# A two-dimensional FFT and a SwiGLU block on one core: buffers drawn by the build-time scheduler, its ScalarE lengths and its priorities set anew

## The chip, the cores and the metric

The kernel runs on one core of a Trainium2 chip. Its time is the device time in microseconds; three runs took 612.49, 616.39 and 612.35 us, with a median of 612.49 us. The engines are TensorE (PE, with its weight loads as PEld), VectorE (DVE), ScalarE (ACT), GpSimd (POOL) and SyncE (SP), which issues the DMAs.

## The reference

```python
def _attn_ref(x):                      # x: (8, 3008, 256) float32
    X = np.fft.fft(x, axis=1)
    X = np.fft.fft(X, axis=2)
    return X.real.astype(np.float32)

def _moe_ref(x, w_gate, w_val, w_out): # x: (24064, 256), w_gate, w_val: (256, 1536), w_out: (1536, 256)
    g = x @ w_gate
    silu = g * (1.0 / (1.0 + np.exp(-g)))
    val = x @ w_val
    return (silu * val @ w_out).astype(np.float32)
```

The real part of a two-dimensional transform of each of the eight batches, reshaped to 24064 rows, goes through a gated feed-forward block.

## The kernel before

**The mathematics in use.** The real part of the transform of a real input has a mirror symmetry. The kernel therefore computes 12032 columns (half the rows of the result) as two parts, `Pt` (even) and `Qt` (odd); row k of the result comes from P + Q and the mirrored row from P - Q. The hidden axis of 256 is folded into the weights once: `Wp` and `Wq` are the gate and value weights times cosine and sine tables, and `Wm` is a multiple of `Wq` for the mirrored rows.

**Tiles and units.** The columns are cut into 24 tiles of 512 (the first of 480, the fourth too, the last of 320 with 8 extra). Each tile has 12 units (t, f), one per 128 of the 1536 hidden values, so there are 288 units. In every unit TensorE makes a gate tile `g` and a value tile `v` in PSUM (512 columns of fp32, one bank each), ScalarE applies Silu, and products `hp` (row) and `hm` (mirrored row) are written as bf16 for the second product with `Wo`. A unit comes in several forms:

- whole (`whole_a`, `whole_b`): six matmuls; ScalarE makes Silu of g twice, VectorE multiplies into hp and hm.
- split (`part_a`, `part_b`): five matmuls. An even value `es` is put aside (by VectorE at L1068 with the broadcast row `bc`, or, in a seeded unit, by a ScalarE copy at L1066 after ScalarE has written the first row into v at L1017). The mirrored value goes by VectorE (L1129) and the mirrored Silu by ScalarE (L1115) into an `sv` tile that serves two units; GpSimd multiplies the pair into hm (L1136). VectorE multiplies hp (L1139), or, in units named by `POOL` and `POOL_END`, ScalarE copies the value (L1145) and GpSimd multiplies (L1148).
- with the gate split too (`GATE...`): one matmul less; VectorE makes an even gate (L1047) and a mirror gate (L1107).

`SPLIT_EARLY`, `GATE_EARLY` (tiles 1 and 2), `SEED`, `POOL`, `GATE` (tiles 3 to 20, in turns of two) and the `..._END` lists (tiles 21 to 23) say which unit has which form.

**The products with Wo.** `OWork` runs the product of the tile before (L1185: eight blocks of 12 matmuls of 256 columns, eight matmuls per unit), ScalarE evicts a pair of blocks from `o` to `ev` (L1191, L1194), and SP stores it (L1197).

**The transform.** For batch b, GpSimd folds the input `XA`, `XC` in twelve steps each (`fold_step`, L162 to L186: SDf, EOf, Af, then CEa/BBa for A or Fc for C). SP loads the input and spreads Fc to `St`. Then `transform_op` multiplies with the tables into an `o` and a `g` tile (L1341), ScalarE copies o to `od` (L1348), and VectorE adds and subtracts into pieces of Pt and Qt (the puts, L1358 and L1364). The first batch, the tables and the weights are made in a prologue of some 22 us.

**Who orders the work.** Every step is an `Op` in a build-time scheduler, `Sched`: an engine, a duration (`act_us`, `dve_us`, `pool_us`, `pe_us` with additions), a lag to other engines (`LAG`), a due time `at` (TensorE's clock at that point plus a shift such as `SH_OD`), and the tiles it opens (`new`). `run` picks for each engine, within a window of due times (`WINDOW`), the step that can start first, and reckons that a tile takes the earliest buffer to come free (`free`). It then calls the steps in that order, and each engine executes its own in order. Pools: three buffers each for g, v, sp, sg and ev, two each for o, sv and es. What buffer a tile gets is left to the pool of that name, which holds all its buffers.

`spread(("C", 1), 6, 6, 12)` and its like (L1230) place the folds by unit; L1526 puts the loads of A1 at unit 8; `ROW_PE` names the units at which TensorE makes the broadcast row of tiles 1 to 3.

Of the kernel before, what the change touches and what calls it, by code (L numbers as in the profile page):

```python
# [31 lines left out]
def kernel(  # L32
# [45 lines left out]
    stp = ctx.enter_context(tc.tile_pool(name="st", bufs=3))  # L78
    pqp = ctx.enter_context(tc.tile_pool(name="pq", bufs=5))
    odp = ctx.enter_context(tc.tile_pool(name="od", bufs=2))  # L80
    psG = ctx.enter_context(tc.tile_pool(name="psG", bufs=3, space=bass.MemoryType.PSUM))
    psV = ctx.enter_context(tc.tile_pool(name="psV", bufs=3, space=bass.MemoryType.PSUM))
    psO = ctx.enter_context(tc.tile_pool(name="psO", bufs=2, space=bass.MemoryType.PSUM))
    ctx.enter_context(tc.manual_schedule())

    Wp = const.tile([P, 2, Dff], BF16, name="Wp")
# [233 lines left out]
    shift = tp.tile([P, 3], F32, name="shift")  # L320
# [355 lines left out]
    for q in range(2):  # L676
        S, Dd = SC[:, 0, :, q, :], SC[:, 1, :, q, :]
# [14 lines left out]
    sgp = ctx.enter_context(tc.tile_pool(name="sg", bufs=3))
    spp = ctx.enter_context(tc.tile_pool(name="sp", bufs=3))
    svp = ctx.enter_context(tc.tile_pool(name="sv", bufs=2))
    esp = ctx.enter_context(tc.tile_pool(name="es", bufs=2))
    brp = ctx.enter_context(tc.tile_pool(name="br", bufs=1))
    bcp = ctx.enter_context(tc.tile_pool(name="bc", bufs=2))
    evp = ctx.enter_context(tc.tile_pool(name="evO", bufs=3))

    def row_pieces(c0, n, minus):  # L700

# [22 lines left out]
        return out[r0:r0 + step * (n - 1) + 1:step, :]  # L724

    ROW_GAP = 1
    LOAD_AT = 2
    LOADS, LOADS_LATER = 4, 3
    SH_ROW = -4
    ES_BUFS = 2  # L730
    SP_BUFS = 3
    SG_BUFS = 3
    EV_BUFS = 3
    W_PE = 9
    W_ACT = 6.25
    W_DVE = 7.25
    W_POOL = 9
    SH_SEED = 4
    SH_EG = 1.45
    SH_SP = 2.85  # L740
    SH_ES = 3.05
    SH_GM = 0.7
    SH_SM = 3.9
    SH_VM = 2.85
    SH_VAL = 0.85
    SH_HP = 3.15
    SH_HM = 3.75
    SH_EV = 4
    SH_FOLD = 3.15
    SH_OD = -2.3  # L750
    SH_PUT = -1.75
    GRP = 4
    WM_ACT = ((1, 0), (1, 1))
    class Op:
        __slots__ = ("eng", "dur", "lat", "fn", "at", "n", "deps", "owners", "new", "ring", "start", "end", "users")

    LAG = {"DMA": 0.0, "PE": 0.20, "ACT": 0.17, "DVE": 0.15, "POOL": 0.12, "SP": 0.0}
    BUFS = {"g": 3, "v": 3, "o": 2, "sp": SP_BUFS, "sv": 2, "es": ES_BUFS, "sg": SG_BUFS, "ev": EV_BUFS, "od": 2, "h": 2, "bc": 2, "br": 1, "pq": 5, "cp": 2,
            "fc": 1, "st": 3}
    WINDOW = {"PE": W_PE, "ACT": W_ACT, "DVE": W_DVE, "POOL": W_POOL, "SP": 6.0, "DMA": 1e9}  # L760
    PSUM = ("g", "v", "o")

    class Sched:

        def __init__(self):
            self.ops = []
            self.wr, self.rd = {}, {}
            self.live = {p: [] for p in BUFS}
            self.clock = 0.0
# [4 lines left out]
        def add(self, eng, dur, fn, r=(), w=(), new=(), after=(), lat=None, shift=0.0, ring=0.35):  # L774
            o = Op()
            o.eng, o.dur, o.fn, o.n = eng, dur, fn, len(self.ops)
            o.lat = LAG[eng] if lat is None else lat
            o.ring = ring
            o.at = self.clock + shift
            if eng == "PE":  # L780
                self.clock += dur
            o.new, o.deps, o.owners = list(new), set(), set()
            for k in r:
                o.owners.add(k[0])
                if k in self.wr:
                    o.deps.add(self.wr[k])
                same = self.rd.setdefault(k, [])
                if k[0][0] in PSUM:
                    o.deps.update(x for x in same if self.ops[x].eng != eng)
                same.append(o.n)  # L790
            for k in after:
                o.deps.update(self.rd.get(k, ()))
            for k in w:
                o.owners.add(k[0])
                if k in self.wr:
                    o.deps.add(self.wr[k])
                o.deps.update(self.rd.pop(k, ()))
                self.wr[k] = o.n
            o.deps.discard(o.n)
            o.owners.update(o.new)  # L800
            self.ops.append(o)

        def run(self, begin):
            ops = self.ops
            last, queue = {}, {p: [] for p in BUFS}
            for o in ops:
# [3 lines left out]
                for w_ in o.new:  # L810
                    if w_ not in queue[w_[0]] and w_ not in self.live[w_[0]]:
                        queue[w_[0]].append(w_)
            free = {p: [0.0] * (BUFS[p] - len(self.live[p])) for p in BUFS}
            owned = {w_ for p in BUFS for w_ in self.live[p]}
            todo = {}
            for o in ops:
# [7 lines left out]
            ring = 0.0  # L824
# [3 lines left out]
            def ready(o):  # L828
                at = 0.0
                for d in o.deps:  # L830
                    x = ops[d]
                    if x.end is None:
                        return None
                    at = max(at, x.end + (x.lat if x.eng != o.eng or x.eng == "SP" else 0.0 if x.eng == "PE" else 0.03))
                for w_ in o.new:
                    if w_ in owned:
                        continue
                    p = w_[0]
                    if queue[p][0] != w_ or not free[p]:
                        return None  # L840
                    at = max(at, min(free[p]))
                return at

            while left:
                best = None
                floor = min(l[0].at for l in todo.values() if l)
                for e, l in todo.items():
# [22 lines left out]
                s, o = best  # L870
# [4 lines left out]
                if o.eng == "SP":  # L875
                    ring = max(o.end + o.lat, ring + o.ring)
                    o.lat = ring - o.end
                    lanes = lanes[1:] + [ring]
                order.append(o)
                for w_ in o.new:  # L880
                    if w_ not in owned:
                        owned.add(w_)
                        queue[w_[0]].remove(w_)
                        free[w_[0]].remove(min(free[w_[0]]))
                for w_ in o.owners:
                    if w_ in last:
# [13 lines left out]
    def act_us(n):  # L900
        return n / 1200 + 0.055
# [9 lines left out]
    state = {}  # L911
    t_end = tile_of((B - 1) * H) + 1
    FIRST = 3 * nF
    ROW_PE = {13: 1, 22: 2, 36: 3}
    SPLIT_EARLY = ((1, 2), (1, 3), (1, 4), (1, 5), (1, 8), (1, 9), (1, 10), (1, 11), (2, 0), (2, 1), (2, 4), (2, 5), (2, 6), (2, 7), (2, 8), (2, 9), (2, 10), (2, 11))
    GATE_EARLY = ((2, 1), (2, 4))

    SEED = (1, 2, 3, 4, 5, 6, 8, 11, 13, 14, 15, 16, 17, 21, 23)
    SEED_END = (0, 4, 6, 8, 9)
    POOL = (16,)  # L920
    POOL_END = (0, 1, 6, 9)
    GATE = (0, 2, 3, 4, 7, 14, 15, 16)
# [24 lines left out]
    S = Sched()  # L947
# [62 lines left out]
    def seed_op(u):  # L1010
        t, f = u
        w = width(t) + (B if t == nT - 1 else 0)
        kv = (("v", u), 0)

        def fn():
            T_[kv] = psV.tile([P, T], F32, name="v")
            nc.scalar.activation(T_[kv][:, :w], bc[t][:, :w], AF.Copy, scale=w0[:, 1, f:f + 1])  # L1017

        S.add("ACT", act_us(w) + 0.13, fn, r=[(("bc", t), 0)], w=[kv], new=[("v", u)], shift=SH_SEED)

    def part_a(u):
        if whole(u):
# [54 lines left out]
    def part_b(u):  # L1077
        if whole(u):
            return whole_b(u)
        t, f = u  # L1080
        w = width(t)
        wp = w + (B if t == nT - 1 else 0)
        kg, kv, kP, kQ = unit_keys(u)
        ksp, kes, keg, kgm = (("sp", u), 0), (("es", u), 0), (("sg", ("eg", u)), 0), (("sg", ("gm", u)), 0)
        ksv = ("sv", (t, f // 2))
# [134 lines left out]
    bc = {}  # L1220
# [375 lines left out]
```

## Time and profile before

| what | value |
|---|---|
| median of three runs | 612.49 us |
| the profiled execution | 612.9 us, of which 611.1 us are the span from first to last instruction |
| granted TensorE clock | 1.00 in every 20 us stretch up to 600 us, 0.96 in the last 11 us |
| ScalarE waits for TensorE's g (L1043, L1115) | 6.3 and 3.7 us |
| GpSimd's hm waits for sv by VectorE and by ScalarE | 37.4 and 28.9 us |
| first matmul of tile 1 and of tile 3 | 44.7 and 95.5 us |
| last matmul | 607.4 us |
| DMA moved | 57.9 MB, 95 GB/s on average |

Busy times are shares of the span. A matmul's own duration in the rows (some 0.38 us for 512 columns) is longer than the distance to the next one, since matmuls are pipelined; distances are taken from start to start. Some 50 of 4066 matmuls have no row in the trace; a gap of exactly one matmul's time is such a row and no wait.

### The profile page before, as it was taken

What the parts mean: (1) busy time and instruction counts of PE and PEld (TensorE: products, weight loads), DVE (VectorE), ACT (ScalarE), POOL (GpSimd) and SP (SyncE); (2) the same over time, 40 slices, a digit from 0 to 9 for tenths busy, and PEclk for the clock granted to TensorE, in tenths of its full rate; (3) what the DMA queues carried; (4) which work ended last, traced back from release to release, by engine and by line L of the source; (5) the groups of instructions that cost most, each with busy time, mean ns of one, the idle gap of its engine ahead of it and who ended that gap; (6) DMA issues with size and microseconds to landing.
All of it is one profiled execution on the core that took longest, in us unless ns stands there. A gap on an engine that the chain in (4) does not pass through costs nothing.

```text
span 611.1 us, 12629 instructions
## 1 busy us (share of the span) xinstructions
PE 597.0 (98%) x4016; PEld 394.9 (65%) x4072; DVE 575.8 (94%) x1066; ACT 558.6 (91%) x1072; POOL 482.3 (79%) x447
## 2 busy tenths in 40 slices
PE   8999999999999999999999999999999999999997
PEld 6556666666666666566666666666666666666676
DVE  8998899999999999989999999999999999998982
ACT  7697679899999999899999999999899999999993
POOL 8847988999899899978897797987886544457662
PEclk9999999999999999999999999999999999999999
DMA  9966337445517234363261113135211212111112
GB/s 227 146 114 145 97 111 176 123 121 139 149 39 166 76 89 137 106 130 100 57 170 52 53 49 93 53 98 134 59 52 36 62 46 63 36 53 51 53 53 79
DMA packets 51055, 57.92 MB, mean 95 GB/s; under 512 B 7254, under 2 KB 38170, under 8 KB 50988
## 3 DMA queue, kind: packets, MB, share of 16 engines
q1 hardware_dynamic: 47334, 53.97, 33.2%
q0 software_dynamic: 3216, 2.36, 2.9%
q10 hardware_dynamic: 438, 0.77, 0.5%
q8 instruction: 32, 0.52, 0.4%
q14 instruction: 35, 0.29, 0.2%
HBM read 29.43 MB, written 24.65 MB: 88 GB/s over the span
## 4 chain that ended last, share of the span: by engine, by line
PE 65%; ACT 9%; DVE 9%; POOL 9%; issue 5%; DMA 1%; POOLq 0%; ACTq 0%; DVEq 0%
PE o L1185 27%; PE g L945 18%; PE v L945 15%; POOL hm L1136 3%; ACT sv L1115 3%; DVE hp L1139 2%; DVE sv L1129 2%; DVE sg L1047 2%; ACT v L1017 2%; DVE sg L1107 1%; ACT es L1066 1%; DMA XA<-in_moe_w_gate_dram 1%; PE o L1341 1%; PE g L1341 1%; ACT sp L1043 1%
## 5 line engine op out<-in xcount | busy, mean ns | idle before, releaser
L1136 POOL TENSOR_TENSOR hm<-sv 128x1024 bf16<-128x1024 f32 (+2 forms) x135 | 251.2, 1862 | 89.0 <-DVE sv L1129 37.4
L1129 DVE SCALAR_TENSOR_TENSOR sv<-es,v 128x512 f32<-128x512 f32 (+2 forms) x270 | 181.4, 673 | 11.3 <-PE v L945 10.1
L1139 DVE TENSOR_TENSOR hp<-sp,v 128x512 bf16<-128x512 f32 (+2 forms) x249 | 167.6, 674 | 2.1 <-ACT sp L1112 1.5
L1185 PE MATMUL o<-Wo,hm 128*128 128x256 bf16 (+1 forms) x1128 | 165.0, 272 | 0.5
L1185 PE MATMUL o<-Wo,hp 128*128 128x256 bf16 (+1 forms) x1104 | 160.6, 272 | 0.8
L1185 PEld LDWEIGHTS <-hm 128*128 128x128 bf16 (+2 forms) x1140 | 111.9, 98 | 60.9 <-issue 1.3
L1185 PEld LDWEIGHTS <-hp 128*128 128x128 bf16 (+2 forms) x1140 | 111.9, 98 | 57.6 <-issue 2.0
L1115 ACT ACTIVATE sv<-g 128x512 f32<-128x512 f32 (+2 forms) x187 | 125.1, 680 | 5.1 <-PE g L945 3.7
L1043 ACT ACTIVATE sp<-g 128x512 f32<-128x512 f32 (+2 forms) x187 | 117.6, 629 | 10.4 <-PE g L945 6.3
L1017 ACT ACTIVATE v<-bc,w 128x512 f32<-128x512 bf16 (+2 forms) x150 | 108.5, 723 | 1.6 <-DVE hp L1139 0.9
L945 PE MATMUL v<-Pt,Wp 128*128 128x512 bf16 (+2 forms) x288 | 106.2, 374 | 1.7 <-DVE hp L1139 0.6
L945 PE MATMUL g<-Pt,Wp 128*128 128x512 bf16 (+2 forms) x277 | 103.4, 374 | 3.2 <-DVE Qt L1358 2.4
L1066 ACT COPY es<-v 128x512 f32<-128x512 f32 (+2 forms) x150 | 91.9, 613 | 1.6 <-PE v L945 0.5
L945 PE MATMUL g<-Qt,Wq 128*128 128x512 bf16 (+2 forms) x247 | 91.5, 374 | 0.4
L1068 DVE SCALAR_TENSOR_TENSOR es<-bc,w,v 128x512 f32<-128x512 bf16 (+2 forms) x120 | 87.6, 731 | 3.4 <-PE v L945 1.8
L945 PE MATMUL g<-Qt,Wm 128*128 128x512 bf16 (+2 forms) x205 | 76.7, 374 | 0.7 <-ACT sp L1043 0.4
L945 PEld LDWEIGHTS <-Wp 128*128 128x128 bf16 x576 | 56.3, 98 | 30.2 <-DVE Qt L1358 2.2
L945 PE MATMUL v<-Qt,Wm 128*128 128x512 bf16 (+2 forms) x165 | 61.9, 375 | 0.4
L1047 DVE SCALAR_TENSOR_TENSOR sg<-bc,w,g 128x512 f32<-128x512 bf16 (+2 forms) x83 | 61.0, 735 | 1.0 <-PE g L945 0.9
L1191 ACT COPY ev<-o 128x512 f32<-128x512 f32 x89 | 55.3, 621 | 6.4 <-PE o L1185 6.0
L945 PEld LDWEIGHTS <-Wq 128*128 128x128 bf16 x426 | 41.6, 98 | 27.1 <-issue 5.4
L1115 ACT ACTIVATE sv<-sg 128x512 f32<-128x512 f32 (+2 forms) x83 | 58.0, 699 | 0.3 <-POOL hm L1136 0.3
(198 smaller groups left out, 743.6 us busy)
## 6 DMA issues: line engine op xcount, KB each, us to landing
out_dram<-ev SPq DMA_DIRECT2D x96, 128.0 KB
XA<-in_x_dram SPq DMA_DIRECT2D x30, 256.0 KB
XA<-in_x_dram SPq DMA_DIRECT2D x112, 64.0 KB
XC<-in_x_dram SPq DMA_DIRECT2D x30, 120.0 KB
XC<-in_x_dram SPq DMA_DIRECT2D x105, 32.0 KB
bc<-br SPq DMA_DIRECT2D x19, 128.0 KB
St<-Fc SPq DMA_DIRECT2D x12, 128.5 KB
out_dram<-ev SPq DMA_DIRECT2D x12, 120.0 KB
```

The source lines that it names most:

```text
L945: nc.tensor.matmul(ps[:, :n], Wt[:, gv, fs], src[:, :n], start=start, stop=stop, skip_group_check=True)
L1017: nc.scalar.activation(T_[kv][:, :w], bc[t][:, :w], AF.Copy, scale=w0[:, 1, f:f + 1])
L1043: nc.scalar.activation(T_[ksp][:, :w], T_[kg][:, :w], AF.Silu)
L1047: nc.vector.scalar_tensor_tensor(T_[keg][:, :w], bc[t][:, :w], w0[:, 0, f:f + 1], T_[kg][:, :w], op0=Alu.mult, op1=Alu.add)
L1066: nc.scalar.copy(T_[kes][:, :w], T_[kv][:, :w])
L1068: nc.vector.scalar_tensor_tensor(T_[kes][:, :w], bc[t][:, :w], w0[:, 1, f:f + 1], T_[kv][:, :w], op0=Alu.mult, op1=Alu.add)
L1115: nc.scalar.activation(sv()[:, f % 2, w - 1::-1, 1], T_[kgm if by_dve else kg][:, :w], AF.Silu)
L1129: nc.vector.scalar_tensor_tensor(sv()[:, f % 2, w - 1::-1, 0], T_[kes][:, :w], 2.0, T_[kv][:, :w], op0=Alu.mult, op1=Alu.subtract)
L1136: nc.gpsimd.tensor_tensor(hts_(t)[1][:, f - 1:f + 1, :w], sv()[:, :, :w, 1], sv()[:, :, :w, 0], op=Alu.mult)
L1139: nc.vector.tensor_tensor(hts_(t)[0][:, f, :wp], T_[ksp][:, :wp], T_[kv][:, :wp], op=Alu.mult)
L1185: nc.tensor.matmul(st["ps"][:n, j, :], hts[t][minus][:, f, c:c + n], Wo[:, f, :], start=(f == 0), stop=(f == nF - 1))
L1191: nc.scalar.copy(ev[:, 0:len(pair), :], st["ps"][:, 0:len(pair), :])
```

## The change

Five things are edited together. (1) Eight pools are replaced by sets of pools with one buffer each (`Slots`), and `run` keeps the number of the buffer that it reckons with, and sets it before the step is called. (2) Three durations and two lags of the planner: seed 0.13 to 0.134, mirrored Silu 0.035 to 0.069 (split gate) and 0.032, ACT's lag 0.17 to 0.18, DVE's 0.15 to 0.145. (3) All shifts and three windows. (4) Which units are split, seeded, on GpSimd or split in the gate, in tiles 1 and 2 and in the last three. (5) The places of the first folds, of A1's loads and of the row of tile 1. Two assertions are added to the planner.

```diff
-    psG = ctx.enter_context(tc.tile_pool(name="psG", bufs=3, space=bass.MemoryType.PSUM))
...
+    class Slots:
+        def __init__(self, name, n, **where):
+            self.pools = [ctx.enter_context(tc.tile_pool(name=f"{name}{i}", bufs=1, **where)) for i in range(n)]
+            self.at = 0
+        def tile(self, *what, **named):
+            t = self.pools[self.at].tile(*what, **named)
+            self.at = (self.at + 1) % len(self.pools)
+            return t
+    psG = Slots("psG", 3, space=bass.MemoryType.PSUM)
...
+    C1_AT = 7
+    A1_AT = 17
+    C2_AT = 34
+    A1_LOAD = 9
+    ROW_1 = 11
...
-    W_PE = 9
-    W_ACT = 6.25
-    W_DVE = 7.25
+    W_PE = 8.5
+    W_ACT = 6.0
+    W_DVE = 8.5
...
-    SH_SEED = 4
-    SH_EG = 1.45
-    SH_SP = 2.85
-    SH_ES = 3.05
-    SH_GM = 0.7
-    SH_SM = 3.9
-    SH_VM = 2.85
-    SH_VAL = 0.85
-    SH_HP = 3.15
-    SH_HM = 3.75
-    SH_EV = 4
-    SH_FOLD = 3.15
-    SH_OD = -2.3
-    SH_PUT = -1.75
+    SH_SEED = 2.75
+    SH_EG = 3.25
+    SH_SP = 1.55
+    SH_ES = 2.85
+    SH_GM = -4
+    SH_SM = 3.25
+    SH_VM = 4
+    SH_VAL = 0.0
+    SH_HP = 4
+    SH_HM = 1.05
+    SH_EV = 2.6
+    SH_FOLD = 1.45
+    SH_OD = -3.75
+    SH_PUT = -4
...
+    SLOTS = {"g": psG, "v": psV, "o": psO, "sp": spp, "sv": svp, "sg": sgp, "es": esp, "ev": evp}
...
-            free = {p: [0.0] * (BUFS[p] - len(self.live[p])) for p in BUFS}
+            free = {p: [(0.0, i) for i in range(len(self.live[p]), BUFS[p])] for p in BUFS}
...
+                        held[w_] = min(free[w_[0]])[1]
                         free[w_[0]].remove(min(free[w_[0]]))
+                        o.slots.append((w_[0], held[w_]))
...
             for o in order:
+                for p, i in o.slots:
+                    if p in SLOTS:
+                        SLOTS[p].at = i
                 o.fn()
...
-    SPLIT_EARLY = ((1, 2), (1, 3), (1, 4), (1, 5), (1, 8), (1, 9), (1, 10), (1, 11), (2, 0), (2, 1), (2, 4), (2, 5), (2, 6), (2, 7), (2, 8), (2, 9), (2, 10), (2, 11))
-    GATE_EARLY = ((2, 1), (2, 4))
+    SPLIT_1 = (0, 1, 2, 3, 4, 5, 6, 7, 8, 9)
+    SPLIT_2 = (0, 1, 2, 3, 4, 5, 8, 9)
+    GATE_2 = (0, 2, 4, 6, 7, 9)
...
-    SEED_END = (0, 4, 6, 8, 9)
+    SEED_END = (4, 5, 7, 10)
...
-    POOL_END = (0, 1, 6, 9)
-    GATE = (0, 2, 3, 4, 7, 14, 15, 16)
-    GATE_END = (0, 3, 6)
+    POOL_END = (0, 6, 7, 9, 10)
+    GATE = (0, 2, 4, 5, 7, 14, 15, 16)
+    GATE_END = (0, 4, 7, 9)
```

A unit of tile 2 has its gate split if it is in both `GATE_2` and `SPLIT_2` (0, 2, 4 and 9). Also changed, though not shown: `SH_ROW` from -4 to 0.15.

More of the change, by code (lines that the diff above doesn't have):

```diff
@@ L80 @@
     odp = ctx.enter_context(tc.tile_pool(name="od", bufs=2))
-    psG = ctx.enter_context(tc.tile_pool(name="psG", bufs=3, space=bass.MemoryType.PSUM))
-    psV = ctx.enter_context(tc.tile_pool(name="psV", bufs=3, space=bass.MemoryType.PSUM))
-    psO = ctx.enter_context(tc.tile_pool(name="psO", bufs=2, space=bass.MemoryType.PSUM))
+    class Slots:
[7 more added lines that the diff above has]
+    psG = Slots("psG", 3, space=bass.MemoryType.PSUM)
+    psV = Slots("psV", 3, space=bass.MemoryType.PSUM)
+    psO = Slots("psO", 2, space=bass.MemoryType.PSUM)
     ctx.enter_context(tc.manual_schedule())
@@ L691 @@
     hp = ctx.enter_context(tc.tile_pool(name="ht", bufs=2))
[L692 to L695, printed above, removed]
+    sgp = Slots("sg", 3)
+    spp = Slots("sp", 3)
+    svp = Slots("sv", 2)
+    esp = Slots("es", 2)
     brp = ctx.enter_context(tc.tile_pool(name="br", bufs=1))
     bcp = ctx.enter_context(tc.tile_pool(name="bc", bufs=2))
-    evp = ctx.enter_context(tc.tile_pool(name="evO", bufs=3))
+    evp = Slots("evO", 3)
     def row_pieces(c0, n, minus):
@@ L726 @@
     ROW_GAP = 1
+    C1_AT = 7
[3 more added lines that the diff above has]
+    ROW_1 = 11
+    ROW_2 = 22
+    ROW_3 = 36
     LOAD_AT = 2
     LOADS, LOADS_LATER = 4, 3
-    SH_ROW = -4
+    SH_ROW = 0.15
     ES_BUFS = 2
@@ L754 @@
     class Op:
-        __slots__ = ("eng", "dur", "lat", "fn", "at", "n", "deps", "owners", "new", "ring", "start", "end", "users")
-    LAG = {"DMA": 0.0, "PE": 0.20, "ACT": 0.17, "DVE": 0.15, "POOL": 0.12, "SP": 0.0}
+        __slots__ = ("eng", "dur", "lat", "fn", "at", "n", "deps", "owners", "new", "ring", "slots", "start", "end", "users")
+    LAG = {"DMA": 0.0, "PE": 0.20, "ACT": 0.18, "DVE": 0.145, "POOL": 0.12, "SP": 0.0}
     BUFS = {"g": 3, "v": 3, "o": 2, "sp": SP_BUFS, "sv": 2, "es": ES_BUFS, "sg": SG_BUFS, "ev": EV_BUFS, "od": 2, "h": 2, "bc": 2, "br": 1, "pq": 5, "cp": 2,
@@ L784, in add @@
                 o.owners.add(k[0])
+                assert k in self.wr or k[0][0] != "bc", k
                 if k in self.wr:
@@ L793, in add @@
             for k in w:
+                assert not (k[0][0] in ("pq", "bc") and self.rd.get(k)), k
                 o.owners.add(k[0])
@@ L812, in run @@
                         queue[w_[0]].append(w_)
-            free = {p: [0.0] * (BUFS[p] - len(self.live[p])) for p in BUFS}
+            free = {p: [(0.0, i) for i in range(len(self.live[p]), BUFS[p])] for p in BUFS}
+            held = {w_: i for p in BUFS for i, w_ in enumerate(self.live[p])}
             owned = {w_ for p in BUFS for w_ in self.live[p]}
@@ L840, in ready @@
                         return None
-                    at = max(at, min(free[p]))
+                    at = max(at, min(free[p])[0])
                 return at
@@ L879, in run @@
                 order.append(o)
+                o.slots = []
                 for w_ in o.new:
@@ L890, in run @@
                             ends = [x.end + x.lat for x in ops if x.end is not None and w_ in x.owners]
-                            free[w_[0]].append(max(ends))
+                            free[w_[0]].append((max(ends), held[w_]))
             for o in order:
+                for p, i in o.slots:
+                    if p in SLOTS:
+                        SLOTS[p].at = i
                 o.fn()
@@ L913 @@
     FIRST = 3 * nF
-    ROW_PE = {13: 1, 22: 2, 36: 3}
-    SPLIT_EARLY = ((1, 2), (1, 3), (1, 4), (1, 5), (1, 8), (1, 9), (1, 10), (1, 11), (2, 0), (2, 1), (2, 4), (2, 5), (2, 6), (2, 7), (2, 8), (2, 9), (2, 10), (2, 11))
-    GATE_EARLY = ((2, 1), (2, 4))
+    ROW_PE = {ROW_1: 1, ROW_2: 2, ROW_3: 3}
+    SPLIT_1 = (0, 1, 2, 3, 4, 5, 6, 7, 8, 9)
+    SPLIT_2 = (0, 1, 2, 3, 4, 5, 8, 9)
+    GATE_2 = (0, 2, 4, 6, 7, 9)
     SEED = (1, 2, 3, 4, 5, 6, 8, 11, 13, 14, 15, 16, 17, 21, 23)
-    SEED_END = (0, 4, 6, 8, 9)
+    SEED_END = (4, 5, 7, 10)
     POOL = (16,)
-    POOL_END = (0, 1, 6, 9)
-    GATE = (0, 2, 3, 4, 7, 14, 15, 16)
-    GATE_END = (0, 3, 6)
+    POOL_END = (0, 6, 7, 9, 10)
+    GATE = (0, 2, 4, 5, 7, 14, 15, 16)
+    GATE_END = (0, 4, 7, 9)
     def whole(u):
-        return u[0] < 3 and u not in SPLIT_EARLY
+        return u[0] < 3 and u[1] not in ((), SPLIT_1, SPLIT_2)[u[0]]
     def seeded(u):
@@ L939, in gate_split @@
         if u[0] < 3:
-            return u in GATE_EARLY
+            return u[0] == 2 and u[1] in GATE_2 and u[1] in SPLIT_2
         return u[0] % 2 * nF + u[1] in GATE if u[0] < t_end else u[1] in GATE_END
@@ L1017, in fn @@
             nc.scalar.activation(T_[kv][:, :w], bc[t][:, :w], AF.Copy, scale=w0[:, 1, f:f + 1])
-        S.add("ACT", act_us(w) + 0.13, fn, r=[(("bc", t), 0)], w=[kv], new=[("v", u)], shift=SH_SEED)
+        S.add("ACT", act_us(w) + 0.134, fn, r=[(("bc", t), 0)], w=[kv], new=[("v", u)], shift=SH_SEED)
     def part_a(u):
@@ L1120, in part_b @@
             S.add("ACT", act_us(wp), silu, r=[kg], w=[ksp], new=[ksp[0]], shift=SH_SP)
-            S.add("ACT", act_us(w) + 0.035, silu_m, r=[kgm], w=[ksm], new=[ksv], shift=SH_SM)
+            S.add("ACT", act_us(w) + 0.069, silu_m, r=[kgm], w=[ksm], new=[ksv], shift=SH_SM)
         else:
-            S.add("ACT", act_us(w) + 0.035, silu_m, r=[kg], w=[ksm], new=[ksv], shift=SH_SM)
+            S.add("ACT", act_us(w) + 0.032, silu_m, r=[kg], w=[ksm], new=[ksv], shift=SH_SM)
         def v2():
@@ L1228, in spread @@
         seq.extend((lo + (i * (hi - lo)) // (n - 1), what, i) for i in range(n))
-    spread(("C", 1), 6, 6, 12)
-    spread(("A", 1), 12, 14, 24)
-    lo = 30
+    spread(("C", 1), 6, C1_AT, C1_AT + 6)
+    spread(("A", 1), 12, A1_AT, A1_AT + 10)
+    lo = C2_AT
     for b in range(2, B, 2):
@@ L1525 @@
             loads.extend((("C", 1), k, fn) for k, fn in enumerate(load_c(1, nc.sync)))
-        if i == 8:
+        if i == A1_LOAD:
             loads[0:0] = ((("A", 1), k, fn) for k, fn in enumerate(load_a(1, nc.sync)))
```

## The prediction

> **What bounds the kernel now.** First the busy times, then the same by 20 us stretches, then the starts of single matmuls where TensorE lags.
>
> ```profile
> PE 597.0 (98%) x4016; PEld 394.9 (65%) x4072; DVE 575.8 (94%) x1066; ACT 558.6 (91%) x1072; POOL 482.3 (79%) x447
> ```
> ```profile
> 160.00:180.00 20.00, 19.89 (x131) 12.83 (x132) 19.92 (x35) 19.44 (x38) 19.55 (x17) 1.00 0.22 64
> ...
> 240.00:260.00 20.00, 18.54 (x119) 11.55 (x119) 19.29 (x34) 18.42 (x37) 19.48 (x18) 1.00 0.45 120
> ...
> 280.00:300.00 20.00, 19.02 (x127) 12.44 (x129) 19.31 (x35) 18.55 (x36) 18.94 (x18) 1.00 0.20 56
> ```
>
> The columns of the stretches are span, busy time of PE, PEld, DVE, ACT, POOL, granted clock, DMA share and GB/s. TensorE bounds: 512 columns start every 0.216 us and 256 every 0.109, without gaps, in nearly every stretch (19.89 of 20 is as full as a row gets). Its idle 14.1 us are 3.1 in the first 40 us, 3.4 behind the last matmul, and a few waits between. VectorE is nearly as full (20.00 of 20 in four stretches).
>
> What the waits between are for is seen at 281.55 us:
>
> ```profile
> 279.57 0.92 DVE L1358 TENSOR_TENSOR Qt<-g,od 128x64 bf16<-128x64 f32 x4
> ...
> 279.75 0.60 ACT L1112 ACTIVATE sp<-g 128x512 f32<-128x512 f32 x1
> ...
> 281.33 0.17 DVE L1358 TENSOR_TENSOR Qt<-g,od 128x12 bf16<-128x12 f32 x1
> ...
> 281.55 0.39 PE L945 MATMUL g<-Pt,Wp 128*128 128x512 bf16 x1 [0.82 <-DVE Qt L1358]
> ```
>
> The new `g` tile takes the PSUM buffer of a transform, whose last read (the 12-column put) ends at 281.50. The buffer that ScalarE had read was free at 280.35. In the built program's addresses the shared pool hands buffers out by another rule than the planner, which reckons with the earliest free one. I went through all g, v and o tiles in this way, with the last read of every buffer from the trace: TensorE stood for a later-freed buffer at 107.1 (0.43 us), 255.7 (0.92), 256.9 (0.71, a `v`), 281.5 (0.93), 355.5 (0.31), 426.9 (0.93), 500.9 (0.32) and twice for 0.07 to 0.08: 4.7 us. At 113.4 ScalarE stood 1.2 us for an `sp` buffer that GpSimd still read while another was free, and TensorE lost 0.60 us behind it at 114.1. Together 5.3 us.
>
> **The change part by part.** *Matmuls.* The new lists of split and gate units take away five: four g<-Qt,Wm of 512 columns and one of 320. 4 x 0.216 + 0.136 = **-1.0 us**, all on TensorE's path.
>
> *Buffers by the planner.* The 5.3 us is the most, zero the least. VectorE limits it: the distance from one instruction's start to the next is at least 0.597 us (L1129, L1139, L1107) and 0.657 (L1068, L1047), and with these its work is 47.2 of the 48.2 us between the tile starts at 266.2 and 314.4, where TensorE waits 0.99. Without that wait both would be full. The stretches 167.8 to 217.1 and 314.4 to 364.0 already hold 49.3 and 49.5 us of VectorE work in 49.2 and 49.6. New waits are also possible. A transform's g tile is held from 1.3 to 3.3 us from its last matmul to its last put; at the old holds, the distances in the new order leave ten of 30 transforms short, by 2.1 us in all (the old order leaves five short, by 3.7). Higher priority of od and puts (SH_OD, SH_PUT) should shorten holds, and the hp that stood between two 7-put groups' puts is gone twice. I take two thirds of 5.3: **-3.5 us**; bounds 0 and -5.3.
>
> *Tile 1.* All units 0 to 9 are now split; before, 0, 1, 6 and 7 were whole. A pair of split units fills one of two `sv` buffers, and a GpSimd product (hm) empties it. GpSimd before:
>
> ```profile
> 49.63 2.35 POOL L162 TENSOR_TENSOR SDf<-XC 128x1020 f32<-128x1020 f32 x1 [12.01 <-DMA XA<-in_x_dram]
> ...
> 54.31 1.10 POOL L172 TENSOR_TENSOR Af<-EOf 128x516 f32<-128x516 f32 x1
> ...
> 58.13 0.73 POOL L1457 MEMSET Tab<- 64x752 bf16 x1
> 58.91 0.73 POOL L1458 MEMSET Tab<- 64x756 bf16 x1
> 59.72 3.75 POOL L1136 TENSOR_TENSOR hm<-sv 128x1024 bf16<-128x1024 f32 x2
> 63.43 2.35 POOL L162 TENSOR_TENSOR SDf<-XA 128x1020 f32<-128x1020 f32 x1
> ```
>
> The fold of C1 starts when its last copy within XC lands. That copy now stands one XA load earlier on SP's queue; issue distances there are 0.4 us, so I leave 49.5. The new order puts hm of units 0 and 1 between EOf and Af: 54.2 to 56.1. The rest of the fold (3.8 us) and the two memsets (1.6) follow, and only then hm of units 2 and 3: 61.5 to 63.4. Units 6 and 7 write the buffer that this hm reads. Their first matmuls end at 58.4 to 58.6 in matmul time counted from tile 1's start (44.7), and an sv write starts some 1.4 us later in the rows of before, so at 59.9; it would now start at 63.4. Both writers stand in ScalarE's and VectorE's queues in the plain order of units, and behind them everything of these engines waits. The g tile of unit 9 takes the buffer that ScalarE's write frees (there are three, all in use): due on TensorE at 61.0, free at 63.4 + 0.65 + 0.2 = 64.2. Cost between 0 and 3.3; nearest to the row sums, **+3.0 us**.
>
> *Moved places.* C1, A1 and C2 folds start one, three and four units later, the row of tile 1 two units earlier. A1's coefficients were written at 80.9 and first used at 88.7. With hm products first and TensorE later too, the sums of GpSimd rows put them near 87 and the use near 91: 0. For batch 2 written 151.6, used 153.0; the same sum comes out level, about 154 both: 0, bounds 0 and +4.5 (rival 3).
>
> *Other engines.* VectorE gains five even gates, five mirror gates and three even values, and loses three products: 6.0 us. Of this 3.5 us lie in the last three tiles, where it idles 5.4 us of 40 (17.95 and 16.66 of 20), and the rest in tiles 1 and 2, where it idles 2.4 of 20 and 0.5 to 1.1 of 20: 0, at most +0.5. ScalarE loses 1.6 us, GpSimd gains 3.4 at the end, where it idles 6 of 20. The last tile's product of unit 10 moves to GpSimd; the closing 36 matmuls from 599.5 reach it 1.1 us in, about when it is written: 0 to +0.6, I take 0.1. The new ScalarE lengths only move the plan. The prologue draws the same buffers in the same turn: 0.
>
> **Sum.** -1.0 - 3.5 + 3.0 + 0.1 = -1.4 us. The profiled execution took 612.9 us (span 611.1), so 611.5 of its like; the median of the runs shown is 0.4 lower: **611.1 us**.
>
> **Rivals.**
> 1. *The wait in tile 1 is not met.* For: VectorE was idle 2.4 us of 20 there, and the copy stands earlier. Against: GpSimd's rows have no gap from 49.6 on. -1.0 - 3.5 = 608.0; with the whole 5.3 us 606.2.
> 2. *The buffers bring nothing*, because VectorE is full or because the plan's ends miss the real ones and a later-freed buffer is still drawn. For: VectorE at 100% in two stretches out of four. Against: VectorE stood idle 0.4 us for TensorE right behind the waits at 281.5 and 426.9. -1.0 + 3.1 = 614.6.
> 3. *Slower: GpSimd's chain to batch 2.* Products are now put ahead of fold steps (SH_HM 1.05 for 3.75), so GpSimd may stand for an sv where it would have folded. A product waited 0.66 us on average (89.0 us over 135). If nine of the products up to 151 us gain such a wait, batch 2's coefficients come 6 us later, and TensorE waits for them at 153; the 1.4 us of slack go first. This decides from 1.4 us of added GpSimd idle time. 611.1 + 4.5 = 615.6. For: GpSimd is busy 19.84 and 19.67 of 20 from 100 to 140. Against: its work up to there hardly changes.
> 4. *The clock.* The wait in tile 1 would be the longest of TensorE; the longest now is 1.4 us at 13.5, and the granted clock is 1.00 in every stretch up to 600 us. The first 52 matmuls of 128 columns took 5.38 us, 103 ns each, nearly what 256 columns take later. Should the array fall back to such a pace for 5 us, half of them is lost: 611.1 + 2.6 = 613.7. [...]
>
> **Chances.** Forecast 0.42, rival 1 0.25, rival 2 0.15, rival 3 0.12, rival 4 0.06. The range runs from rival 1 with most of its buffers, 606.5, to rival 3, 616.0. 1% is 6.1 us, about what a measurement here tells from no change: under 606.4 lies only the end of rival 1 (0.08), over 618.6 the end of rival 3 (0.05), the rest is 0.87.
>
> **What would show it.** Right: no TensorE wait of 0.9 us near 255, 281 and 427, a PE wait of about 3 us at 61 with ScalarE's and VectorE's sv writes waiting for hm, GpSimd's second hm not before 61, VectorE at 99% of the stretches that had 97%. Wrong: no wait at 61, or waits at the old places for a put or an sv write, or a transform's matmul that waits for CEa.

## The result and the profile after

The changed kernel took **605.65 us** (median of four runs, 605.42 to 606.99) beside 612.62 us of the kernel before on the same chip: a ratio of 0.9877, 95% interval 0.9836 to 0.9917. In a later series it took 604.99 us beside 613.02: 0.9862, interval 0.9841 to 0.9883. It is some 7 to 8 us faster, just more than 1%. The prediction was 611.1 us with a range from 606.5 to 616.0; it was wrong. (Medians of one kernel differ by about half a microsecond between the series.)

The profiled execution after took 605.58 us, with a span of 603.8. The busy times and the 20 us stretches that answer to those of before:

```profile
PE 593.0 (98%) x4010; PEld 394.2 (65%) x4067; DVE 578.4 (96%) x1076; ACT 555.6 (92%) x1069; POOL 485.4 (80%) x450
```
```profile
160.00:180.00 20.00, 19.89 (x134) 13.07 (x134) 19.73 (x35) 19.22 (x38) 18.77 (x16) 1.00 0.18 55
240.00:260.00 20.00, 19.84 (x131) 12.85 (x133) 19.75 (x36) 19.93 (x40) 19.77 (x18) 1.00 0.47 124
280.00:300.00 20.00, 19.89 (x136) 13.22 (x137) 20.00 (x34) 19.62 (x38) 18.37 (x16) 1.00 0.23 63
```

TensorE's second column went from 18.54 to 19.84 and from 19.02 to 19.89: the two stretches that held the waits are as full as the one that had none. The list of TensorE's waits (engine, line, what it waited for: total us, times, longest) says the same; nothing of it belongs to a put of the main part, and the first four lines lie in the first 40 us:

```profile
PE g L427 <- DVE SA L436: 1.6, 1, 1.6
PE o L299 <- DVE sel L247: 1.0, 1, 1.0
PE o L1418 <- DMA XA<-in_moe_w_gate_dram: 0.7, 1, 0.7
PE o L1418 <- DMA XA<-in_moe_w_val_dram: 0.5, 1, 0.5
PE v L974 <- DVE hp L1168: 0.2, 1, 0.2
PE g L974 <- ACT sv L1144: 0.2, 1, 0.2
PE g L974 <- DVE Qt L641: 0.2, 1, 0.2
```

GpSimd in tile 1, the place where the prediction put 3.0 us:

```profile
47.36 2.35 POOL L174 TENSOR_TENSOR SDf<-XC 128x1020 f32<-128x1020 f32 x1 [9.33 <-DMA XA<-in_x_dram]
...
53.07 1.90 POOL L1165 TENSOR_TENSOR hm<-sv 128x1024 bf16<-128x1024 f32 x1 [1.11 <-ACT sv L1144]
...
60.34 3.75 POOL L1165 TENSOR_TENSOR hm<-sv 128x1024 bf16<-128x1024 f32 x2
```

The order is the predicted one. The fold begins 2.3 us earlier than before, and hm of units 2 and 3 (the last row) at 60.3 us instead of the predicted 61.5.

To add TensorE up without gaps in the records, I took from start to start of its matmuls what exceeds (columns + 6)/2.4 ns, a line through the distances seen in full stretches (0.216 us for 512 columns, 0.109 for 256; twice that, 0.43 us for 512 columns, for the twelve matmuls of fp32 operands at the start). The kernel before has 4072 matmuls, as the full trace of `slots_only` (below), which has its order, shows; 56 of them have no row in its own trace. After there are 4067, and 57 without a row. All of these have 512 columns, and their time is put in. This **lost time**, in us of the profiled executions, is used below:

| kernel | first 44 us | behind 44 us |
|---|---|---|
| before | 6.34 | 9.88 |
| after / after once more | 7.24 / 6.94 | 2.65 / 3.26 |
| before's order, all buffers by the planner | 5.79 | 4.29 |
| before's order, PSUM buffers alone by the planner | 6.86 | 5.19 |
| after's order, shared pools | 6.47 | 11.08 |

The span fell by 7.3: 7.2 of lost time behind 44 us and 1.0 of matmuls, less 0.9 in the start. That 0.9 is not shown to be the change's. TensorE's order up to 41 us is the same in all of these runs and those below, and still their lost time in the first 44 us lies between 5.8 and 7.4 us, mostly by one wait at 13 us (0.8 to 2.1 us).

### The profile page after: what moved, and what is told of

Read it like the earlier page. It is cut to its first block, busy times and chain, and to the rows that moved or that the text cites. A ratio compares the mean times of both kernels' runs of the same rounds, so it can differ in the third digit from the quotient of the medians.

```text
span 603.8 us, 12560 instructions
## 1 busy us (share of the span) xinstructions
PE 593.0 (98%) x4010; PEld 394.2 (65%) x4067; DVE 578.4 (96%) x1076; ACT 555.6 (92%) x1069; POOL 485.4 (80%) x450
## 4 chain that ended last, share of the span: by engine, by line
PE 90%; POOL 3%; issue 2%; DMA 2%; DVE 2%; ACT 2%; ACTq 0%; DVEq 0%; POOLq 0%
PE o L1214 39%; PE g L974 24%; PE v L974 20%; PE g L1370 2%; PE o L1370 2%; DMA XA<-in_moe_w_val_dram 2%; PE o L299 1%; PE v L1214 1%; POOL hm L1165 1%; POOL EOA L493 1%; ACT sv L1144 1%; PE g L599 0%; DVE sv L1158 0%; DVE hp L1168 0%; ACT sp L1072 0%
## 5 line engine op out<-in xcount | busy, mean ns | idle before, releaser
L1168 DVE TENSOR_TENSOR hp<-sp,v 128x512 bf16<-128x512 f32 (+2 forms) x246 | 165.0, 671 | 0.2 <-ACT sp L1141 0.2
L1144 ACT ACTIVATE sv<-g 128x512 f32<-128x512 f32 (+2 forms) x182 | 120.0, 677 | 4.3 <-POOL hm L1165 1.9
L1072 ACT ACTIVATE sp<-g 128x512 f32<-128x512 f32 (+2 forms) x182 | 113.5, 627 | 4.5 <-PE g L974 2.5
L974 PE MATMUL g<-Pt,Wp 128*128 128x512 bf16 (+2 forms) x281 | 105.2, 374 | 0.8 <-ACT sv L1144 0.2
L1097 DVE SCALAR_TENSOR_TENSOR es<-bc,w,v 128x512 f32<-128x512 bf16 (+2 forms) x123 | 89.2, 726 | 2.9 <-PE v L974 1.4
L974 PE MATMUL g<-Qt,Wm 128*128 128x512 bf16 (+2 forms) x196 | 73.3, 374 | 0.3
L1076 DVE SCALAR_TENSOR_TENSOR sg<-bc,w,g 128x512 f32<-128x512 bf16 (+2 forms) x88 | 64.3, 730 | 0.2
L1144 ACT ACTIVATE sv<-sg 128x512 f32<-128x512 f32 (+2 forms) x88 | 63.1, 720 | 0.3 <-DVE sg L1136 0.3
L1141 ACT ACTIVATE sp<-g 128x512 f32<-128x512 f32 (+2 forms) x88 | 55.9, 636 | 4.8 <-DVE sg L1136 4.5
```

The costliest lines, as they stand in the source:

```text
L974: nc.tensor.matmul(ps[:, :n], Wt[:, gv, fs], src[:, :n], start=start, stop=stop, skip_group_check=True)
L1072: nc.scalar.activation(T_[ksp][:, :w], T_[kg][:, :w], AF.Silu)
L1076: nc.vector.scalar_tensor_tensor(T_[keg][:, :w], bc[t][:, :w], w0[:, 0, f:f + 1], T_[kg][:, :w], op0=Alu.mult, op1=Alu.add)
L1097: nc.vector.scalar_tensor_tensor(T_[kes][:, :w], bc[t][:, :w], w0[:, 1, f:f + 1], T_[kv][:, :w], op0=Alu.mult, op1=Alu.add)
L1141: nc.scalar.activation(T_[ksp][:, :wp], T_[kg][:, :wp], AF.Silu)
L1144: nc.scalar.activation(sv()[:, f % 2, w - 1::-1, 1], T_[kgm if by_dve else kg][:, :w], AF.Silu)
```

## The experiments

### Buffers alone, and all but the buffers

`slots_only` is the kernel before with edit (1) alone; every engine's order is that of before. `rest_only` is the changed kernel with its order, and shared pools. What the new durations, edit (2), and the moved places, edit (5), bring by themselves was not tried.

```diff
# rest_only, against the changed kernel (and likewise for the seven other pools)
-    psG = Slots("psG", 3, space=bass.MemoryType.PSUM)
+    psG = ctx.enter_context(tc.tile_pool(name="psG", bufs=3, space=bass.MemoryType.PSUM))
...
-                    if p in SLOTS:
+                    if False:
```

> The kernel before with the pools of one and the planner's choice of buffers alone; every engine's order, the lists, the lengths and the priorities are those of before. Theory A (the changed kernel's trace: TensorE's gaps between 100 and 560 us went from 8.56 to 1.59 us, VectorE at 99 to 100% of the stretches without a lag): most of the gain is this, 607.0 us, 5.0 to 6.5 faster than before; no TensorE wait over 0.3 us near 107, 255, 281, 427 and 500 us. Theory B (the prediction's: VectorE's work limits the stretches, so a third of the waits comes back elsewhere): 609.0 us. Theory C (the waits go, but it is the new order with its higher priority of the puts that keeps new ones away): 610 to 612.5 us, with TensorE waits for a put at other times.

> The changed kernel with its order of every engine kept, but its eight pools shared as before, so that the pool picks the buffer. Theory A (buffers bring 5.0 to 6.0 us, the rest 1.0 by five matmuls and little else): 610.5 to 611.5 us, with TensorE waits of 0.3 to 0.9 us in which a later-freed buffer is drawn. Theory C (the order brings the gain, the choice of buffers little): 606 to 607 us. If the new order draws more unluckily than the old: over 612.5 us.

Measured: `slots_only` **606.61 us** (ratio 0.9904, 0.9891 to 0.9917), `rest_only` **611.75 us** (0.9992, 0.9980 to 1.0004). TensorE's waits of `slots_only`, all that are listed:

```profile
PE o L298 <- DVE sel L246: 1.0, 1, 1.0
PE g L426 <- DMA XC<-in_x_dram: 0.7, 1, 0.7
PE o L1408 <- DMA XA<-in_moe_w_val_dram: 0.4, 1, 0.4
PE o L1408 <- ACT Wm L1417: 0.3, 1, 0.3
PE v L964 <- DVE sv L1148: 0.2, 1, 0.2
PE g L964 <- DVE Qt L640: 0.2, 1, 0.2
```

The largest of `rest_only`:

```profile
PE g L974 <- ACT sv L1144: 2.1, 3, 1.6
PE v L974 <- DVE hp L1168: 1.8, 2, 1.0
PE g L974 <- DVE Qt L1387: 1.4, 2, 0.7
PE g L427 <- DMA XC<-in_x_dram: 1.3, 1, 1.3
PE o L299 <- DVE sel L247: 1.0, 1, 1.0
PE g L974 <- ACT sp L1141: 1.0, 1, 1.0
```

In the first list no main-part wait is over 0.2 us. In the second the waits for a put (Qt, L1387) are back, at 282.46 and 426.96 us, nearly where the kernel before had them (281.55 and 426.9), and new ones for hp at 209.7 and 212.2. So 5.9 of the 7 us come from the choice of the buffer. This is theory A of `slots_only`, 0.4 us better than it said. The new order without it is within the measurement of no change (0.25 us above theory A of `rest_only`): its five saved matmuls (1.0 us) go into 1.2 us more of lost time.

### PSUM tiles and work buffers apart

`slots_psum` gives the planner's choice to g, v and o only.

```diff
-    SLOTS = {"g": psG, "v": psV, "o": psO, "sp": spp, "sv": svp, "sg": sgp, "es": esp, "ev": evp}
+    SLOTS = {"g": psG, "v": psV, "o": psO}
```

> The kernel before with the planner's choice for g, v and o alone; sp, sv, sg, es and ev stay shared. The prediction's split: 4.7 us of TensorE's waits are for PSUM tiles and 0.6 for an sp buffer, so 607.2 to 607.8 us, with ScalarE's wait of 1.2 us at 113 and TensorE's 0.6 at 114 still there. If the work buffers matter more than the sp wait showed (through ScalarE at 567 and 582, 0.4 and 0.5 us): up to 608.5.

Measured: 608.79 us (0.9938, 0.9918 to 0.9958), 0.3 us above the upper end of what was expected. ScalarE at 113.67:

```profile
113.67 0.57 ACT L1062 ACTIVATE sp<-g 128x480 f32<-128x480 f32 x1 [1.65 <-POOL hp L1167]
```

The wait for GpSimd is still there (1.65 us, in `slots_only` 0.34 and for another reason), and TensorE loses 1.0 us behind it at 114.3. By the lost time behind 44 us the PSUM tiles bring 9.88 - 5.19 = 4.7, the work buffers 0.9 more. The medians put 2.2 us between the two kernels; 1.1 of the 2.0 in their spans lie in the first 44 us, within the scatter that this part has in all runs. So how much of the medians' 2.2 us is the work buffers' stays open.

### The wait in tile 1

`fold_twice` and `fold_thrice` do the first step of C1's fold two and three times over, so that GpSimd is later by 2.4 and 4.9 us and nothing else changes. `memset_later` moves 1.5 us of memsets on GpSimd behind the hm products that TensorE depends on. `after_again` is the changed kernel itself.

```diff
# fold_twice (range(2) in fold_thrice), in fold_step
+            if what == ("C", 1) and j == 0:
+                for _ in range(1):
+                    queue[what][0]()
             queue[what].pop(0)()
# memset_later
-              17: [lambda: S.add("POOL", 0.8, halve_tables, w=[(("Tab",), "z")])],
+              20: [lambda: S.add("POOL", 0.8, halve_tables, w=[(("Tab",), "z")])],
```

> The changed kernel in which GpSimd does the first step of C1's fold (SDf and its last column) twice, so that all behind it on GpSimd comes 2.4 to 2.5 us later; nothing else moves. Theory A (tile 1 goes as the prediction wrote it: hm of units 2 and 3 lets ScalarE and VectorE write sv of units 6 and 7, and TensorE waits for the g that ScalarE frees; in the changed kernel's trace this chain reaches TensorE at 63.0 with nothing to spare): +2.2 to +2.5 us, 607.8 to 608.2 us, a TensorE wait of 2 us or more near 64. Theory B (tile 1 has cover of its own that the trace does not show): 605.5 to 606.2 us and no wait over 0.5 us.

> The same with the step done three times, 4.9 us later. Theory A: +4.6 to +5 us, 610.2 to 610.7 us, one TensorE wait of some 4.5 us or two that add up to it near 64 to 66, and full pace behind it. Theory E (the prediction's rival on the clock: a pause of this length costs pace afterwards): matmuls of 512 columns at up to twice their 0.216 us for some us behind the wait, 612 to 613 us. Theory B: under 608 us.

> The changed kernel once more, unchanged, for its spread. Theory A (its order leaves tile 1 no slack: C1's second copy was issued at 41.2 us and the fold began at 47.4 us in its trace, at 42.8 and 49.6 in the run with shared pools, which has the same order): a median of 605.5 to 606.5 us; a profile in which the fold begins after 49 us has a TensorE wait of 1 to 2 us near 64, one in which it begins by 48 us has none over 0.3.

> The changed kernel with the two memsets of the table's halves (1.5 us on GpSimd) put behind the second and third hm product of tile 1 instead of ahead of them; the other engines' orders are the same. Theory A (tile 1's chain through GpSimd is what is left to lose there): hm of units 2 and 3 ends 1.5 us earlier for the same start of the fold, no TensorE wait over 0.3 us near 64 even with a fold that begins at 49.5, and a median at or up to 0.6 us under that of the changed kernel. Theory B (no loss there in most executions): the same median within 0.2 us.

Measured: 607.39, 610.38, 604.99 and 604.69 us. `fold_twice` and `fold_thrice` were timed together (ratios 0.9909, 0.9881 to 0.9936, and 0.9965, 0.9941 to 0.9988), the other two together (0.9862 and 0.9860, not to be told apart). The rows of `fold_thrice` at the wait:

```profile
63.52 0.60 PE L1214 MATMUL o<-Wo,hm 128*128 128x256 bf16 x4
67.10 0.38 PE L974 MATMUL g<-Pt,Wp 128*128 128x512 bf16 x1 [2.97 <-ACT sv L1144]
67.31 0.38 PE L974 MATMUL g<-Qt,Wq 128*128 128x512 bf16 x1
67.74 0.38 PE L974 MATMUL v<-Pt,Wp 128*128 128x512 bf16 x1
```

And GpSimd and TensorE in `rest_only`, which has the changed order:

```profile
49.56 2.35 POOL L174 TENSOR_TENSOR SDf<-XC 128x1020 f32<-128x1020 f32 x1 [12.00 <-DMA XA<-in_x_dram]
...
61.38 3.75 POOL L1165 TENSOR_TENSOR hm<-sv 128x1024 bf16<-128x1024 f32 x2
```
```profile
64.00 0.38 PE L974 MATMUL g<-Pt,Wp 128*128 128x512 bf16 x1 [1.56 <-ACT sv L1144]
```

With these, every execution of the changed order obeys one sum. The g of unit 9 is due 17.18 us after the first matmul of tile 1, and its buffer is free 2.62 us after hm of units 2 and 3 starts (1.87 for the product, the rest for ScalarE's sv write and the lags). All in us:

| kernel | C1 copy issued | fold begins | tile 1 begins | g due | hm starts | g free | wait by the sum | wait in the trace |
|---|---|---|---|---|---|---|---|---|
| predicted | | 49.5 | 44.7 | 61.0 | 61.5 | 64.2 | 3.2 | |
| after | 41.25 | 47.36 | 45.86 | 63.04 | 60.34 | 62.96 | 0 | 0 |
| after once more | 41.82 | 48.94 | 45.56 | 62.74 | 60.76 | 63.38 | 0.64 | 0.63 |
| rest_only | 42.81 | 49.56 | 45.09 | 62.27 | 61.38 | 64.00 | 1.73 | 1.72 |
| fold_twice | 41.20 | 48.21 | 46.06 | 63.24 | 62.51 | 65.13 | 1.89 | 1.88 |
| fold_thrice | 40.92 | 47.71 | 45.43 | 63.96 | 64.48 | 67.10 | 3.14 | 3.14 |
| memset_later | 40.84 | 47.79 | 45.97 | 63.15 | 58.87 | 61.49 | 0 | 0 |
| dve_cast (below) | 41.87 | 47.65 | 44.78 | 61.96 | 59.47 | 62.09 | 0.13 | 0.14 |
| dve_after (below) | 42.00 | 48.42 | 44.40 | 61.58 | 60.25 | 62.87 | 1.29 | 1.28 |

(`fold_thrice` is due 1.35 us later, since it lost that at 59.8 to the product before.) Up to 0.2 us more follows, for hp. So the mechanism is the predicted one, and its price depends on the execution: the copy was issued between 40.8 and 42.8 us, and the fold began 5.8 to 7.1 us later. The median of `fold_thrice` is where theory A had it, that of `fold_twice` 0.4 us under it, and that of `after_again` 0.5 us under what it said; the wait of 0.63 us there belongs to a fold that began at 48.9, between the two cases that were named. Theory B falls; the cover that theory A denied is there in some executions, by chance of the DMAs, and `memset_later` provides it by order, which the medians are too coarse to show.

### The lists and the priorities

`old_lists` puts the lists of before into the changed kernel, `old_shifts` all its shifts and windows.

```diff
# old_lists
-    SPLIT_1 = (0, 1, 2, 3, 4, 5, 6, 7, 8, 9)
+    SPLIT_EARLY = ((1, 2), (1, 3), (1, 4), (1, 5), (1, 8), (1, 9), (1, 10), (1, 11), (2, 0), ...
...
# old_shifts
-    SH_HM = 1.05
+    SH_HM = 3.75
...
```

> The changed kernel with the lists of split, gate, seeded and GpSimd units of before; buffers, lengths, priorities and places are the changed ones. Theory A (the lists bring their five matmuls, and no more): 606.6 to 606.8 us. Theory F (units 0, 1, 6 and 7 of tile 1 whole again take away the sv pair that TensorE stood for by up to 1.7 us in the run with shared pools): 605.3 to 606.0 us. If VectorE's work of the three end tiles had limited them: under 605.3.

> The changed kernel with all shifts and windows of before; buffers, lists, lengths and places are the changed ones. Theory A (the buffers brought the gain, and the priorities move little): 605.4 to 607.2 us; the old order with the buffers alone had 1.7 us more of TensorE's gaps behind 44 us than the changed kernel, so +1.6 is the most. Theory G (lists and places need the new priorities): over 607.5 us, with TensorE waits in tile 1, tile 2 or behind 560 us.

Measured, in one series: `old_lists` **606.05 us** (0.9881, 0.9850 to 0.9911), `old_shifts` **608.84 us** (0.9921, 0.9892 to 0.9950). With the old lists tile 1 loses nothing (0.02 us of lost time from 44 to 100, after 0.45 and 1.16), but there are 1.1 us of new waits at 152 to 156 us, two of them for ScalarE (es and v), and its lost time behind 44 us, 3.00, lies between the changed kernel's 2.65 and 3.26. By the traces the lists thus bring about their five matmuls (1.0 us). The median lies 0.05 us above theory F's range and 0.55 under theory A's, and the medians are too coarse to tell the two apart. With the old priorities the lost time behind 44 us is 5.72 instead of 2.65, of which 2.7 us more lie between 44 and 150 us: theory G. The new lists, places and durations lose 3.4 us in that stretch with the old priorities, and the old ones 1.3 (`slots_only`).

### VectorE's room

The prediction held that VectorE would limit what the waits give back. Two edits add VectorE work that no one needs:

```diff
# dve_before, dve_after (behind product_p)
+            if f == 5 and 2 < t < nT - 1:
+                for _ in range(2):
+                    nc.vector.tensor_tensor(SDt, SDt, SDt, op=Alu.mult)
# dve_cast
+                for c in range(2):
+                    nc.vector.tensor_copy(SDt[:, c], T_[kv][:, c * P:(c + 1) * P])
```

> The kernel before with two more VectorE products of 256 columns in each of the tiles 3 to 22, a table that nothing reads any more multiplied by itself, right behind the product of unit 5; some 0.33 us each, 13 us in all. Over tiles 6 to 20 VectorE's smallest distances add up to 332.0 of 341.5 us, so 9.5 us are free there and 9.9 us are added. Theory A (these distances are the floor, and what stands free can be used): +1 to +3 us. Theory B (the added work delays what TensorE waits for, wherever it falls): +8 to +13 us. Theory D (the floor is lower than the distances): 0.

> The changed kernel with the same 40 products. Its VectorE distances add up to 331.9 of 336.2 us over tiles 6 to 20, so 4.3 us are free and 9.9 us are added. Theory A (the distances are the floor, so VectorE binds the changed kernel just below TensorE): +5 to +9 us, with the stretches of tiles 6 to 20 at 100% of VectorE and TensorE waiting for its reads. Theory D (TensorE alone binds and VectorE has room that the distances hide): 0 to +1 us.

> The changed kernel with two VectorE casts of 128 columns out of PSUM (the value tile) in each of the tiles 3 to 22, right behind the product of unit 5, written to a table that nothing reads any more; no second SBUF operand, so no turn with GpSimd as the 256-column products of the earlier run had it. Estimate from the rows of 128 and 188 columns: 0.2 us each from start to start, 8 us in all, 6 us of it over tiles 6 to 20, where 4.3 are free. Theory A (VectorE's distances are a floor, and free time is used): +2 to +4 us. Theory B (work late by 0.4 us reaches TensorE every time): +7 to +9 us. Theory D (VectorE has room that the distances hide): 0 to +1 us.

Measured: 649.85 us (1.0618, 1.0595 to 1.0642), 649.36 us (1.0608, 1.0569 to 1.0646) and **611.48 us** (0.9975, 0.9958 to 0.9991). The first two missed all expectations, since the products did not have the 0.33 us that the author had estimated. The tile's rows (duration min/median/max in ns, first and last start):

```profile
L1142 DVE TENSOR_TENSOR SDt<-SDt x40: 279/1072/2322, 111.8 to 609.4; 128x256 bf16<-128x256 bf16 x40
```

In `dve_before` they added 43.9 us of VectorE time instead of 13, and the kernel became 37.4 us slower. Some 3.4 us of that are two stretches of 3.41 us at half the granted clock (an estimate, half of each; the end tells of them). They say nothing of 10 us more or less (the end has rows of them). In `dve_cast` all the added instructions are short:

```profile
L1171 DVE CAST SDt<-v x40: 281/284/291, 111.6 to 570.6; 128x128 bf16<-128x128 f32 x40
```

VectorE's work in the tiles 6 to 20, by the smallest usual distances of its instructions (the tenth percentile for each form), is 331.9 of 336.2 us in the changed kernel. The casts make it 337.3, and the same tiles take 340.2: 5.4 us added where 4.3 were free cost 4.0. The stretch of two tiles that was 99.8% full (49.06 us) grows by 0.71 of 0.80 added, one at 96.9% (47.31) by 0.30 of 0.77. The whole kernel is 6.5 us slower than the changed one in the same series (4.9 between the profiled executions), between theories A and B: VectorE's work limits the kernel just below TensorE's, and free time in one stretch does not wholly serve the next. The casts also read a v tile, and so could hold its buffer longer; of TensorE's listed waits one of 0.2 us is for a cast, and five of together 0.8 us are for the es behind it.

## Why the prediction was wrong

Three terms of the sum were off, all to the same side: the buffers by 2.1 us, tile 1 by 2.2 to 2.9 us, and the order, which had no term, by 1.8 us. The start, 0.9 us longer in the profiled execution, hid some of it.

**Matmuls (-1.0): right.** Five rows fewer, in a span that TensorE bounds.

**Buffers: the mechanism was right, the term was made too small for a false reason.** The waits counted in the trace of before, 4.7 us for PSUM tiles and 5.3 with sp, came out as 4.7 and 5.6 when they were removed alone. The step that failed is "VectorE limits it ... I take two thirds": -3.5 should have been the whole. "Its work is 47.2 of the 48.2 us" in the stretch from 266.2 is too high; counted again as above it is 46.7. And the waits lay where VectorE had room: the stretches with the waits of 0.7 to 0.9 us were 93.2% (from 217.1), 96.8% (from 266.2) and 96.7% (from 411.6) full; the fuller ones, on which the argument leant, held 0.3 us at most. (These shares move by up to 1% with how the instructions are grouped for the count.) The floor is real, as `dve_cast` shows, but it was not reached: after the change it is at 99.8% in the fullest stretches. "New waits are also possible ... by 2.1 us" did not come; with the old order and the buffers alone there were none over 0.35 us behind 44 us.

**Tile 1 (+3.0): the mechanism was right, two sizes were off.** It cost 0.14 us in the profiled execution and 0.85 in the second, with what follows for hp. The steps that failed are "I leave 49.5" for the fold, which began at 47.4 and 48.9 (49.6 with shared pools, and there hm started at 61.4 and g was free at 64.0, as predicted), and "due on TensorE at 61.0": the matmul time from tile 1's start was 17.2 us, not 16.3, and the tile began at 45.9 instead of 44.7. Of the bounds 0 to 3.3 I took the upper end as if the row sums fixed both arrivals; one hangs on a DMA that scatters by 2 us, the other on a start that scatters by 1.7.

**Order (0): missed.** With the buffers given, the new order lost 1.0 to 1.6 us less behind 44 us than the old (4.29 against 3.26 and 2.65); that is 1.8 us in both, when tile 1's wait is taken off. The prediction had no term for it, and `old_shifts` shows that it hangs on the priorities. Which of them was not tried. The small terms (places and other engines 0, the end +0.1) were not tried alone either; the lost time behind 560 us went from 0.81 to 0.61.

**Rivals.** The first, with the whole 5.3 us (606.2), is nearest to what happened; it had a chance of 0.25 and the range began 0.3 above it. That it comes so near is in part luck, since it has no term for the order's 1.8 us, nor for the 0.9 us of the start, which went the other way. "Buffers bring nothing" is refuted by `slots_only`. GpSimd's chain to batch 2 (rival 3) did not come up: the lost time between 100 and 150 us fell from 1.44 to 0.30. The clock (rival 4) did not come up in tile 1: after the longest pause there, 2.97 us in `fold_thrice`, the next 512-column matmuls start 0.21 us apart and the granted clock is 1.00. This is no rule for a pause of 3 us. In `dve_before` and `dve_after` the granted clock fell to 0.50 after pauses of 2.0 to 2.8 us, and did not after one of 3.82 us; the end has the rows. No run shows the 5 us at a slow pace behind a pause that the rival reckoned with; each of these stretches at 0.50 lasted 3.41 us.

**Signs.** No wait of 0.9 us near 255, 281 and 427, as said. VectorE at 99% in the stretches that had 97%, as said (98.9% in the two tiles from 263.2), and still the gain was whole: that sign did not tell the two cases apart. The wait at 61 and the second hm not before 61 were wrong in the changed kernel's own trace, right with shared pools.

## What to carry to other kernels

Where a planner picks buffers, check that the built program draws the ones it reckoned with: comparing each tile's buffer with the last read of all buffers of its pool gave, from the trace of before alone, the gain to within 0.3 us. Before you discount a gain because another engine is full, count that engine's work in the very stretches that hold the waits, from start to start, not in the fullest ones. Where a wait is the difference of two arrivals, write both as sums with their scatter over several executions; one trace fixes neither where a DMA is in the sum.

## What the runs showed of the hardware

The added 256-column products of two bf16 operands in SBUF took 0.28 to 0.37 us in 13 of the 40 cases of `dve_before`, and up to 2.32 us in the others. Rows of `dve_before`:

```profile
161.14 2.18 DVE L1142 TENSOR_TENSOR SDt<-SDt 128x256 bf16<-128x256 bf16 x2
161.18 2.00 POOL L1136 TENSOR_TENSOR hm<-sv 128x1024 bf16<-128x1024 f32 x1 [0.36 <-ACT sv L1115]
163.14 2.40 POOL L162 TENSOR_TENSOR SDf<-XA 128x1020 f32<-128x1020 f32 x1
163.25 0.73 DVE L1068 SCALAR_TENSOR_TENSOR es<-bc,w,v 128x512 f32<-128x512 bf16 x1
```

All of the other 27 ended 0.14 to 0.16 us after a GpSimd instruction did; in `dve_after` 28 of 28. In the rows above, the second product ends at 163.33, with hm gone at 163.18: it took 1.87 us, and the next VectorE instruction, es, starts at 163.25. The kernel's own hp products (512 columns of fp32, one operand in PSUM) show nothing of the kind: in the trace of before they took 0.68 us on average, both the 150 that ran wholly beside GpSimd work and the 12 that ran wholly without it. What held the long products is not shown beyond these times.

The granted clock fell to 0.50 twice in `dve_before` (at 193.10 and 326.22 us) and twice in `dve_after` (at 377.78 and 456.28), for 3.41 us each. Matmuls of 512 columns then start 0.43 us apart instead of 0.216. In `dve_after`, a short pause with a drop behind it, and the longest pause between two matmuls in all runs, without one:

```profile
377.56 0.40 PE L974 MATMUL v<-Pt,Wp 128*128 128x512 bf16 x1 [2.19 <-ACT v L1046]
377.78 0.61 PE L974 MATMUL v<-Qt,Wq 128*128 128x512 bf16 x1
378.18 0.63 PE L974 MATMUL g<-Pt,Wp 128*128 128x512 bf16 x1
378.61 0.63 PE L974 MATMUL g<-Qt,Wq 128*128 128x512 bf16 x1
```
```profile
378.00:380.00 2.00, 2.00 (x8) 1.02 (x7) 1.83 (x4) 1.71 (x5) 1.81 (x1) 0.50 0.10 28
```
```profile
246.59 0.38 PE L974 MATMUL v<-Qt,Wq 128*128 128x512 bf16 x1 [3.82 <-DVE es L1097]
246.80 0.60 PE L1217 MATMUL o<-Wo,hm 128*128 128x256 bf16 x4
247.24 0.38 PE L974 MATMUL g<-Qt,Wm 128*128 128x512 bf16 x1
```

The four drops stood behind pauses of 2.0 to 2.8 us: 2.77 us, ending at 191.79, ahead of the first in `dve_before`, and 2.19 us in the first rows above. The pause of 3.82 us had no drop behind it, nor had that of 2.97 us in `fold_thrice`. So the length of a pause alone does not tell these cases apart; what does was not tried.
